# Clustered attention into a gated MLP: second projection's weights staged later, low parts on POOL, more buffers, sums on PE

## The chip, the cores and the metric

One Trainium2 chip, one core. The time is that of one execution on the device, in microseconds; lower is better. The core has five engines that run side by side and wait for each other by semaphores: PE (TensorE, matmul), DVE (VectorE), ACT (ScalarE), POOL (GpSimd) and SP (SyncE, which here only issues DMAs). PEld is PE's weight load, which overlaps its matmuls. Every engine works through its own list of instructions in the order of the list: an instruction that waits holds up all that stand behind it.

## The reference

Shapes: q, k, v are (batch 4, heads 8, sequence 768, head size 64); there are 16 centroids per head.

```python
q_assign = np.argmax(np.einsum('bhsd,hcd->bhsc', q_n, c_n), axis=-1)   # normalised q, k, centroids
k_assign = np.argmax(np.einsum('bhsd,hcd->bhsc', k_n, c_n), axis=-1)
mask = q_assign[:, :, :, None] == k_assign[:, :, None, :]
scores = np.where(mask, scale * np.matmul(q, k.transpose(0, 1, 3, 2)), -1000000000.0)
attn = np.exp(scores - np.max(scores, axis=-1, keepdims=True))
attn = attn / (np.sum(attn, axis=-1, keepdims=True) + 1e-09)
x = np.matmul(attn, v)                                   # heads side by side: (4, 768, 512)

h = np.maximum(x @ w_in, 0.0)                            # w_in (512, 1024)
u, v = (h[..., :d_ff // 2], h[..., d_ff // 2:])          # 512 columns each
v_n = (v - mu) / np.sqrt(var + 1e-06)                    # over the 512 columns
v_s = np.einsum('ts,bsd->btd', w_spatial, v_n) + b_spatial[None, :, None]
return ((u * v_s) @ w_out).astype(np.float32)            # w_out (512, 512)
```

w_in and w_out arrive as 64-bit floats, which DVE turns into 32-bit ones by three instructions on their 32-bit words.

## The kernel before, in words

**Numbers.** Nearly every matmul operand is held as two f16 parts, a high part (the value rounded to f16) and a low part (the value less the high part), and a product is three matmuls: high by high, high by low, low by high. So each tile that feeds PE costs a cast on one engine and a subtraction on another. ACT mostly makes the high parts, and POOL or DVE the low ones.

**Attention.** The 32 heads go in 16 pairs; pairs 0 to 3 are the first batch, 4 to 7 the second. For a pair, `prep` loads `raw` (k and q, transposed) and `vraw`, splits them into `hq`/`lo` (L532 on ACT, L538 on DVE) and `vhl` (L601 on ACT, L606 on DVE; for the first two pairs L604 on POOL), assigns clusters on DVE (L566 to L578), and forms the column sums of v that the rows without a key in their cluster need. These sums come in two ways. For pairs 0 to 3 PE multiplies a tile of ones with the split v (L613 and L614, 12 matmuls). For later pairs (`short`) DVE adds the six blocks of `vraw` into `vs` (L621), and PE adds over the partitions in one f32 matmul (L622). `shifts` computes scores once for their row maxima: PE L662 into a PSUM bank `acc`, DVE's maximum `nm` (L669), 18 to a head. `attend` then does for each of a head's six key tiles the scores (PE, L713 and L715, into `sc`), exp (ACT, L719, `p`), the high part (ACT, L721) and the low part (POOL, L722) of `pt`, and the values (PE, L727, 18 matmuls). A head ends with DVE's `rc` (L746), the first instruction on its finished values: there are 32, and the texts count progress by them. `xhl` is the head's result as two parts, and a DMA turns a pair's into `xT`.

**MLP.** For a batch, `mlp` makes six v tiles (12 matmuls each against the second half of `win`; ACT's relu into `v32`, DVE's mean and variance L798 to L812, `vn` in two parts, the low one by POOL, L813), six u tiles (first half of `win`), six s tiles (18 matmuls against `wsp`, then DVE's L832, L833 and POOL's L834, and a DMA that transposes `ghl` into `gT`) and six p tiles (12 matmuls against `wou`, ACT's L842 into `o32`, and an output DMA that ACT issues, L843). All big MLP matmuls have line L771 (a helper). MLP tiles of a batch are spread among the next batch's attention; the last batch's have nothing to stand among.

**Weights.** `weights` (from L450) stages a weight: load; for the 64-bit ones DVE's L477, L478, L479 (into `top`, which for `w_in` is a PSUM bank `acc`); ACT's L461 for the high part; DVE's L462 for the low part. `w_in` is loaded into the buffer that later holds `vn`, four tiles for its second half (columns of v), then four for its first (columns of u). `early_weights` gives times for its loads from `W_AT` on, `W_GAP` apart; `late_weights` stages `wsp` (12 tiles) and `wou` (8 tiles) from `WL_AT` on.

**Order.** The kernel plans its own order. `Plan.run` goes through the operations by estimated costs, and at each free engine takes, of those that are ready, the one with the lowest `due` time plus `key`. The result is one fixed list for each engine, in which the SP queue (nearly all loads, and the transposes) is one more in-order list. Whoever changes a cost, a key or a number of buffers changes the lists everywhere.

**Buffers.** `o32` has 1, `v32` 2 (`MV_BUFS`), `u32` 4; `acc` four PSUM banks and `sc` two double ones. PE, DVE's maxima, the MLP and the staging of `w_in` share the four banks.

Of the kernel before, what the change touches and what calls it, by code (L numbers as in the profile page):

```python
# [69 lines left out]
K_RC = -1.64  # L70
K_XD = 3.66
K_X = -1.98
K_VT = -3.58
K_G = -9.5
KP0 = -16.99
# [200 lines left out]
def kernel(  # L276
# [175 lines left out]
    def weights(jobs, at, gap, key, raws, tops, on, after=()):  # L452
        ends = []
        for m, (src, dst, n, lg, wide, cell) in enumerate(jobs):
# [3 lines left out]

            def lows(x, ld, n=n, dst=dst, sc=sc, raw=raw, cell=cell, use=()):

                h = op("ACT", 0.2 + 0.00085 * n, lambda: A.activation(out=dst()[:, 0, :], in_=x(), func=AF.Copy, scale=sc), after=ld, use=use, key=key)  # L461
                lo = op("DVE", (0.05 if n > 384 else 0.4) + 0.00125 * n, lambda: V.scalar_tensor_tensor(out=dst()[:, 1, :], in0=x(), scalar=sc, in1=dst()[:, 0, :], op0=ALU.mult, op1=ALU.subtract), after=[h], use=use, key=key)  # L462
                w_ops.setdefault(cell, []).extend([h, lo])
                ends.append(lo)
# [51 lines left out]
    def prep(n):  # L516
# [98 lines left out]

        short = n >= NPR
        m = D if short else D + 1
        unit = MEAN_UNIT * (V_SCALE if short else 1.0)
        if short:
            vs = r_vs.new()  # L620
            o = op("DVE", 0.9, lambda: V.tensor_reduce(out=vs.t, in_=vraw.t.rearrange("p t c -> p c t"), axis=AX.X, op=ALU.add), after=[ldv], use=[vraw], new=[vs], key=KV)  # L621
            o = op("PE", 0.4, lambda: T.matmul(out=sv.t[0:2, 0:2 * (D + 2)].rearrange("p (h d) -> p h d", h=2)[:, :, 0:D], lhsT=one32, rhs=vs.t.rearrange("p (h d) -> p h d", h=2), start=True, stop=True), after=[o, c_wh], use=[vs], new=[sv], cols=512, key=KV)  # L622
# [136 lines left out]
    vn_read = [[] for _ in range(NT)]  # L759

    def mlp(b):
        plan.due = None
# [25 lines left out]
        def v_tile(t, pos):  # L788
# [21 lines left out]
            for k, t, v in ((0, t - 1, vs[0]), (1, t, vs[1])):  # L810
                o = op("DVE", 0.62, lambda k=k, v=v: V.tensor_scalar(out=v.t, in0=v.t, scalar1=mv.t[:, k, 0:1], scalar2=y.t[:, k:k + 1], op0=ALU.subtract, op1=ALU.mult), after=[yo], use=[v, mv, y], key=1)
                h = op("DVE", 0.41, lambda t=t, v=v: V.tensor_copy(out=vn[:, 0, t, :], in_=v.t), after=[o] + vn_read[t], use=[v], key=1)  # L812
                l = op("POOL", 1.3, lambda t=t, v=v: G_.tensor_tensor(out=vn[:, 1, t, :], in0=v.t, in1=vn[:, 0, t, :], op=ALU.subtract), after=[h], use=[v], key=1)  # L813
# [23 lines left out]
        def p_tile(t, tr, pos):  # L837
# [4 lines left out]
            o = op("ACT", 0.57, lambda: A.activation(out=o32.t, in_=acc.t, func=AF.Copy, scale=2.0 ** -(G_LOG + WOUT_LOG)), after=[o], use=[acc], new=[o32], key=-0.7)  # L842
            op("ACT", 0.06, lambda: A.dma_start(out=out[b, t * P:(t + 1) * P, :], in_=o32.t), after=[o], use=[o32], dma=0.8, key=0)  # L843

# [69 lines left out]
```

## Time and profile before

| what | us |
|---|---|
| median of 3 runs (690.49 to 691.19) | 691.05 |
| the profiled execution | 694.26 |
| its span, first to last instruction | 692.5 |
| PE, DVE, ACT, POOL busy in the span | 637.5, 482.0, 437.7, 435.3 |
| mean granted PE clock | 0.985 |

The profiled execution is one of its own, 3.2 us longer than the median of the runs. The page lists a matmul's whole duration, and matmuls are pipelined: an instruction that is listed with 379 ns is followed by the next after 216 ns. So a busy PE need not be a full PE; what PE could do is better read from how fast matmuls follow each other where nothing holds them. DVE's and ACT's listed durations also overlap, by less. The granted clock counts for PE alone.

### The profile page before, as it was taken

How to read it: one execution, taken by the hardware profiler on the slowest of the kernel's cores; microseconds unless marked ns; L12 is line 12 of the kernel's file. 1: busy time of each engine (PE TensorE's matmuls, PEld its weight loads, DVE VectorE, ACT ScalarE, POOL GpSimd, SP SyncE). 2: the span in 40 equal slices, each digit the busy share in tenths (PEclk: the TensorE clock that was granted, in tenths of full speed). 3: DMA queues.
4: the chain of work that ended last, by engine and by line, in shares of the span. 5: the costliest groups of instructions: out<-in, count | busy, mean ns of one | idle time of the engine just before them, and what ended most of it. 6: DMA issues, size and time to landing. Idle time of an engine off the chain costs nothing.

```text
span 692.5 us, 16725 instructions
## 1 busy us (share of the span) xinstructions
PE 637.5 (92%) x6757; PEld 379.0 (55%) x6757; DVE 482.0 (70%) x940; ACT 437.7 (63%) x685; POOL 435.3 (63%) x305
## 2 busy tenths in 40 slices
PE   2978889999998999988799899999999999999996
PEld 1456566666555655555445556556655655544442
DVE  6999989998969889999754877558485821215210
ACT  5686889998848756678443966667673957412111
POOL 2485778998949667677363976767665966703210
PEclk9998999999999799999999999999999999999999
DMA  5567665574634467442831536262510113140223
GB/s 165 147 154 213 147 107 142 137 168 116 138 110 82 97 165 167 109 116 60 189 61 36 150 74 137 61 152 50 120 34 1 37 28 70 32 115 0 31 61 92
DMA packets 106515, 70.49 MB, mean 102 GB/s; under 512 B 90379, under 2 KB 93126, under 8 KB 106438
## 3 DMA queue, kind: packets, MB, share of 16 engines
q1 hardware_dynamic: 102694, 62.74, 40.4%
q10 hardware_dynamic: 3744, 6.69, 2.7%
q8 instruction: 53, 0.87, 0.5%
q14 instruction: 24, 0.20, 0.1%
HBM read 27.63 MB, written 6.29 MB: 49 GB/s over the span
## 4 chain that ended last, share of the span: by engine, by line
PE 60%; DVE 20%; ACT 9%; issue 5%; DMA 4%; POOL 2%; POOLq 0%; SPq 0%; ACTq 0%; DVEq 0%
PE acc L771 35%; PE acc L727 9%; DVE nm L669 8%; PE acc L662 6%; PE sc L713 5%; PE sc L715 5%; ACT p L719 4%; ACT pt L721 3%; DVE lo L538 2%; POOL pt L722 2%; DMA out_dram<-o 2%; DMA gT<-ghl 1%; ACT hq L532 1%; DVE vhl L606 1%; DVE acc L568 1%
## 5 line engine op out<-in xcount | busy, mean ns | idle before, releaser
L722 POOL TENSOR_TENSOR pt<-p,pt 128x768 f16<-128x768 f32 x192 | 329.7, 1736 | 103.1 <-ACT pt L721 50.6
L719 ACT ACTIVATE p<-sc,plog 128x768 f32<-128x768 f32 x192 | 168.9, 898 | 58.4 <-PE sc L715 53.8
L669 DVE TENSOR_REDUCE nm<-acc 128x1 f32<-128x512 f32 (+1 forms) x288 | 179.8, 683 | 12.4 <-PE acc L662 12.0
L721 ACT CAST pt<-p 128x768 f16<-128x768 f32 x192 | 155.6, 828 | 12.9 <-PE acc L727 11.1
L727 PE MATMUL acc<-vhl,pt 128*128 128x65 f16 (+1 forms) x3456 | 139.2, 196 | 7.6 <-POOL pt L722 6.9
L727 PEld LDWEIGHTS <-pt 128*128 128x128 f16 x3456 | 129.1, 99 | 30.3 <-POOL pt L722 10.1
L771 PE MATMUL acc<-win,xT 128*128 128x512 f16 x576 | 130.0, 379 | 0.0
L662 PE MATMUL acc<-hq 80*128 80x256 f16 (+1 forms) x384 | 101.1, 339 | 20.7 <-DVE nm L669 10.1
L713 PE MATMUL sc<-hq,lo 128*128 128x512 f16 (+1 forms) x384 | 95.7, 331 | 6.3 <-ACT p L719 6.1
L715 PE MATMUL sc<-hq 81*128 81x512 f16 (+1 forms) x384 | 96.0, 331 | 1.0 <-DMA hq<-sht 1.0
L771 PE MATMUL acc<-vn,wsp 128*128 128x512 f16 x432 | 96.8, 379 | 0.0
L771 PEld LDWEIGHTS <-xT 128*128 128x128 f16 x576 | 54.9, 98 | 63.2 <-issue 0.7
L771 PEld LDWEIGHTS <-wsp 128*128 128x128 f16 x432 | 41.8, 98 | 48.9 <-issue 0.2
L834 POOL TENSOR_TENSOR ghl<-u,ghl 128x512 f16<-128x512 f32 x24 | 27.7, 1156 | 64.0 <-DVE ghl L833 49.2
L832 DVE SCALAR_TENSOR_TENSOR u<-acc,bsp,u 128x512 f32<-128x512 f32 x24 | 17.9, 747 | 71.5 <-PE acc L771 71.5
L771 PE MATMUL acc<-wou,gT 128*128 128x512 f16 x288 | 65.6, 379 | 1.7 <-DMA gT<-ghl 1.7
L662 PEld LDWEIGHTS <-hq 80*128 80x128 f16 x384 | 35.3, 99 | 43.2 <-issue 25.1
L538 DVE SCALAR_TENSOR_TENSOR lo<-raw,hq 128x768 f16<-128x768 f32 x30 | 44.9, 1505 | 12.4 <-ACT hq L532 12.0
L713 PEld LDWEIGHTS <-lo 128*128 128x128 f16 x384 | 34.1, 98 | 34.9 <-issue 20.8
L715 PEld LDWEIGHTS <-hq 81*128 81x128 f16 x384 | 37.9, 99 | 27.7 <-issue 2.7
L842 ACT ACTIVATE o<-acc 128x512 f32<-128x512 f32 x24 | 14.3, 597 | 57.0 <-PE acc L771 41.2
L771 PEld LDWEIGHTS <-gT 128*128 128x128 f16 x288 | 27.7, 98 | 33.8 <-DMA gT<-ghl 2.2
(111 smaller groups left out, 628.5 us busy)
## 6 DMA issues: line engine op xcount, KB each, us to landing
raw<-in_kqT_dram SPq DMA_DIRECT2D x15, 768.0 KB
vraw<-in_vp_dram SPq DMA_DIRECT2D x16, 384.0 KB
out_dram<-o ACTq DMA_DIRECT2D x24, 256.0 KB
hq<-hq SPq DMA_DIRECT2D x15, 384.0 KB
vn<-in_w_in_dram SPq DMA_DIRECT2D x8, 512.0 KB
hq<-lo SPq DMA_DIRECT2D x16, 192.0 KB
lo<-hq SPq DMA_DIRECT2D x16, 192.0 KB
wraw<-in_wsT_dram SPq DMA_DIRECT2D x12, 192.0 KB
```

The lines of the kernel that those rows point to most:

```text
L538: los.append(op("DVE", 1.4 if n else 0.96, lambda h=h: V.scalar_tensor_tensor(out=lo.t[:, h, :], in0=raw.t[:, h, :], scalar=QK_SCALE, in1= ...
L662: T.matmul(out=acc.t[:, c:c + cs.stop - cs.start], lhsT=hq.t[0:R_SH, 1, h, t * P:(t + 1) * P], rhs=hq.t[0:R_SH, 0, h, cs], start=c == 0, s ...
L669: V.tensor_reduce(out=nm.t[:, t, k:k + 1] if n == 1 else nm.t[:, t:t + n, k], in_=src, axis=AX.X, op=ALU.max, negate=True)
L713: T.matmul(out=sc.t[:, cs], lhsT=lo.t[:, h, ks], rhs=hq.t[:, 2, h, cs], start=True, stop=False)
L715: T.matmul(out=sc.t[:, cs], lhsT=hq.t[0:R_E, 0, h, ks], rhs=hq.t[0:R_E, 1, h, cs], start=False, stop=True)
L719: o = op("ACT", 0.9, lambda sc=sc, p32=p32: A.activation(out=p32.t, in_=sc.t[:, 0:S], func=AF.Exp, bias=plog, scale=SC_UNIT), after=[o, m_ ...
L721: o = op("ACT", 0.83, lambda pt=pt, p32=p32: A.copy(out=pt.t[:, 0, :], in_=p32.t), after=[o], use=[p32], new=[pt], key=K_HI)
L722: o = op("POOL", 1.72, lambda pt=pt, p32=p32: G_.tensor_tensor(out=pt.t[:, 1, :], in0=p32.t, in1=pt.t[:, 0, :], op=ALU.subtract), after=[o ...
L727: T.matmul(out=av.t[:, t * (D + 1):t * (D + 1) + w], lhsT=lhsT, rhs=rhs, skip_group_check=True, **f)
L771: T.matmul(out=acc.t, lhsT=lr[m][0], rhs=lr[m][1], start=(m == 0), stop=(m == n - 1))
L832: o = op("DVE", 0.72, lambda: V.scalar_tensor_tensor(out=u32.t, in0=acc.t, scalar=bsp[:, t:t + 1], in1=u32.t, op0=ALU.add, op1=ALU.mult), ...
L834: l = op("POOL", 1.2, lambda: G_.tensor_tensor(out=ghl.t[:, 1, :], in0=u32.t, in1=ghl.t[:, 0, :], op=ALU.subtract), after=[h], use=[u32, g ...
```

## The change

- `early_weights` gets a second time: the tiles of the second half of `w_in` (v) load from `W_AT` on, those of the first half (u) from `W2_AT` on. Since the loads use `vn`'s buffer, the first batch's `vn` now waits for the end of both (`staged`).
- The low parts of `wsp` go from one DVE instruction (L462) to two: ACT scales the loaded tile in place, and POOL subtracts the high part.
- `o32` has 2 buffers, `v32` 3.
- `short` begins at pair 8: pairs 4 to 7 take their sums of v on PE, and DVE's `vs` and the f32 matmul fall away for them.
- Four estimates of cost are changed, and most of the keys and due times. The instructions of the attention and of the MLP stay what they were, in another order.

```diff
-MV_BUFS = 2
+MV_BUFS = 3
-W_KEY = 7.7
-WL_KEY = 0.91
-W_AT = 28.34
-W_GAP = 5.52
+W_KEY = 5.13
+WL_KEY = 1.28
+W_AT = 26.85
+W2_AT = 112.97
+W_GAP = 5.89
...
-K_LO = 2.77
+K_LO = 6.27
...
-    r_o32 = R(moe, "o32", [P, DM], F32, 1)
+    r_o32 = R(moe, "o32", [P, DM], F32, 2)
...
                 h = op("ACT", 0.2 + 0.00085 * n, lambda: A.activation(out=dst()[:, 0, :], in_=x(), func=AF.Copy, scale=sc), after=ld, use=use, key=key)
-                lo = op("DVE", (0.05 if n > 384 else 0.4) + 0.00125 * n, lambda: V.scalar_tensor_tensor(out=dst()[:, 1, :], in0=x(), scalar=sc, in1=dst()[:, 0, :], op0=ALU.mult, op1=ALU.subtract), after=[h], use=use, key=key)
+                if not wide:
+                    o = op("ACT", 0.2 + 0.00085 * n, lambda: A.activation(out=x(), in_=x(), func=AF.Copy, scale=sc), after=[h], use=use, key=key)
+                    lo = op("POOL", 0.1 + 0.0021 * n, lambda: G_.tensor_tensor(out=dst()[:, 1, :], in0=x(), in1=dst()[:, 0, :], op=ALU.subtract), after=[o], use=use, key=key)
+                else:
+                    lo = op("DVE", (0.05 if n > 384 else 0.4) + 0.00125 * n, lambda: V.scalar_tensor_tensor(out=dst()[:, 1, :], in0=x(), scalar=sc, in1=dst()[:, 0, :], op0=ALU.mult, op1=ALU.subtract), after=[h], use=use, key=key)
...
     def early_weights():
-        jobs = []
-        for hf in (1, 0):
+        ends = []
+        for hf, at in ((1, W_AT), (0, W2_AT)):
+            jobs = []
...
-        return weights(jobs, W_AT, W_GAP, W_KEY, r_wraw0, r_acc, "SP")
+            ends += weights(jobs, at, W_GAP, W_KEY, r_wraw0, r_acc, "SP")
+        return ends
...
-        short = n >= NPR
+        short = n >= 2 * NPR
...
+    def staged():
+        return w_ops[("win", 0)] + w_ops[("win", 1)]
...
-                h = op("DVE", 0.41, lambda t=t, v=v: V.tensor_copy(out=vn[:, 0, t, :], in_=v.t), after=[o] + vn_read[t], use=[v], key=1)
+                h = op("DVE", 0.41, lambda t=t, v=v: V.tensor_copy(out=vn[:, 0, t, :], in_=v.t), after=[o] + vn_read[t] + (staged() if b == 0 else []), use=[v], key=1)
```

What the lists show of it, at three places. First DVE, at the end of the fourth head. Before, the last two tiles of the u half stand there (`acc<-vn` are the three word instructions, `win` the low part), in front of the head's `rc`:

```order
L477 TENSOR_SCALAR acc_114<-vn 128x512
L477 TENSOR_SCALAR acc_113<-vn 128x512
L478 SCALAR_TENSOR_TENSOR acc_114<-vn,acc_114 128x512
L478 SCALAR_TENSOR_TENSOR acc_113<-vn,acc_113 128x512
L479 SCALAR_TENSOR_TENSOR acc_114<-vn,acc_114 128x512
L479 SCALAR_TENSOR_TENSOR acc_113<-vn,acc_113 128x512
L462 SCALAR_TENSOR_TENSOR win<-acc_114,win 128x512
L462 SCALAR_TENSOR_TENSOR win<-acc_113,win 128x512
L746 TENSOR_SCALAR rc<-acc_115 128x6
```

In the change the same instructions (with new line numbers: L482 to L484 and L467) stand around the `rc` of the eighth head, among a later pair's maxima `nm`:

```order
L676 TENSOR_REDUCE nm_91<-acc_112 128x1
L482 TENSOR_SCALAR acc_115<-vn 128x512
L676 TENSOR_REDUCE nm_91<-acc_113 128x2
L483 SCALAR_TENSOR_TENSOR acc_115<-vn,acc_115 128x512
L482 TENSOR_SCALAR acc_113<-vn 128x512
L484 SCALAR_TENSOR_TENSOR acc_115<-vn,acc_115 128x512
L483 SCALAR_TENSOR_TENSOR acc_113<-vn,acc_113 128x512
L545 SCALAR_TENSOR_TENSOR lo<-raw,hq 128x768
L484 SCALAR_TENSOR_TENSOR acc_113<-vn,acc_113 128x512
L753 TENSOR_SCALAR rc<-acc_114 128x6
L467 SCALAR_TENSOR_TENSOR win<-acc_115,win 128x512
```

The u half has moved from the third and fourth heads to the seventh to ninth. Second, POOL at the twelfth head, where the first batch's v tiles are normalised (`vn`). Before:

```order
L813 TENSOR_TENSOR vn<-v_3351,vn 128x512
L813 TENSOR_TENSOR vn<-v_3387,vn 128x512
L722 TENSOR_TENSOR pt<-p_3506,pt 128x768
L805 TENSOR_TENSOR y<-a,mhalf 128x2
L722 TENSOR_TENSOR pt<-p_3559,pt 128x768
L722 TENSOR_TENSOR pt<-p_3581,pt 128x768
L813 TENSOR_TENSOR vn<-v_3489,vn 128x512
```

In the change (L729 is `pt`, L816 `y`, L824 `vn`, L465 the moved low part):

```order
L824 TENSOR_TENSOR vn<-v_3361,vn 128x512
L824 TENSOR_TENSOR vn<-v_3386,vn 128x512
L465 TENSOR_TENSOR wsp<-wraw,wsp 128x384 x2
L816 TENSOR_TENSOR y<-a,mhalf 128x2
L465 TENSOR_TENSOR wsp<-wraw,wsp 128x384
L824 TENSOR_TENSOR vn<-v_3486,vn 128x512
L824 TENSOR_TENSOR vn<-v_3520,vn 128x512
L465 TENSOR_TENSOR wsp<-wraw,wsp 128x384
L729 TENSOR_TENSOR pt<-p_3601,pt 128x768
L729 TENSOR_TENSOR pt<-p_3626,pt 128x768
L465 TENSOR_TENSOR wsp<-wraw,wsp 128x384
```

Five of the twelve stand before the twelfth head's last `pt`, all twelve before the fourteenth's. Third, ACT at the first batch's p tiles. Before, three results stand with one exp among them:

```order
L842 ACTIVATE o_5517<-acc_114 128x512
L843 DMA out_dram<-o_5517 128x512
L842 ACTIVATE o_5577<-acc_113 128x512
L843 DMA out_dram<-o_5577 128x512
L719 ACTIVATE p_5584<-sc_111,plog 128x768
L721 CAST pt<-p_5584 128x768
L842 ACTIVATE o_5636<-acc_112 128x512
L843 DMA out_dram<-o_5636 128x512
```

In the change (L853 and L854 are the result and its DMA, L726 exp, L728 the high part, L688 and L691 small rows of the shift):

```order
L853 ACTIVATE o_5091<-acc_112 128x512
L854 DMA out_dram<-o_5091 128x512
L853 ACTIVATE o_5108<-acc_113 128x512
L854 DMA out_dram<-o_5108 128x512
L726 ACTIVATE p_5164<-sc_110,plog 128x768
L728 CAST pt<-p_5164 128x768
L688 ACTIVATE shx_86<-nl 128x6
L691 ACTIVATE shx_86<-nl,flag 128x6 x2
L726 ACTIVATE p_5211<-sc_111,plog 128x768
L728 CAST pt<-p_5211 128x768
L757 CAST xhl<-xn 128x6x64
L853 ACTIVATE o_5233<-acc_113 128x512
```

Two results still stand in a row, but with two buffers the second needs no landing of the first, and the third stands two exps further on. The first p tiles also come earlier: ACT's first result stands in the eighteenth head instead of the nineteenth.

More of the change, by code (lines that the diff above doesn't have):

```diff
@@ L42 @@
 DUE = 25.06
-DUE_PREP = -1.8
+DUE_PREP = -1.88
 DUE_MAX = -0.66
-DUE_M = 31.24
+DUE_M = 31.37
 DUE_W = 1.2
@@ L49 @@
 V_BUFS = 2
-MV_BUFS = 2
+MV_BUFS = 3
 U_BUFS = 4
 MM = 6
-W_KEY = 7.7
-WL_KEY = 0.91
-WL_AT = 183.98
-WL_GAP = 3.25
-W_AT = 28.34
-W_GAP = 5.52
-PREP_KEY = 2.81
-AV_KEY = 1.09
-K_SC = -2.4
+W_KEY = 5.13
+WL_KEY = 1.28
+WL_AT = 183.63
+WL_GAP = 3.35
+W_AT = 26.85
+W2_AT = 112.97
+W_GAP = 5.89
+PREP_KEY = 2.55
+AV_KEY = 1.25
+K_SC = -2.21
 K_MX = -2.81
-K_MAX = -0.27
+K_MAX = -2.18
 TBL = 0.14
-K_SH = -3.11
-K_EXP = 0.71
-K_HI = -1.78
-K_LO = 2.77
[L70 to L74, printed above, removed]
+K_SH = -3.05
+K_EXP = -0.75
+K_HI = -1.44
+K_LO = 6.27
+K_RC = -2.97
+K_XD = 3.02
+K_X = -3.85
+K_VT = -2.01
+K_G = -9.74
 KP0 = -16.99
@@ L457, in weights, with lows @@
             t0 = at + gap * m
-            def lows(x, ld, n=n, dst=dst, sc=sc, raw=raw, cell=cell, use=()):
+            def lows(x, ld, n=n, wide=wide, dst=dst, sc=sc, raw=raw, cell=cell, use=()):
                 h = op("ACT", 0.2 + 0.00085 * n, lambda: A.activation(out=dst()[:, 0, :], in_=x(), func=AF.Copy, scale=sc), after=ld, use=use, key=key)
-                lo = op("DVE", (0.05 if n > 384 else 0.4) + 0.00125 * n, lambda: V.scalar_tensor_tensor(out=dst()[:, 1, :], in0=x(), scalar=sc, in1=dst()[:, 0, :], op0=ALU.mult, op1=ALU.subtract), after=[h], use=use, key=key)
+                if not wide:
[3 more added lines that the diff above has]
+                    lo = op("DVE", (0.05 if n > 384 else 0.4) + 0.00125 * n, lambda: V.scalar_tensor_tensor(out=dst()[:, 1, :], in0=x(), scalar=sc, in1=dst()[:, 0, :], op0=ALU.mult, op1=ALU.subtract), after=[h], use=use, key=key)
                 w_ops.setdefault(cell, []).extend([h, lo])
@@ L537, in prep @@
                 continue
-            los.append(op("DVE", 1.4 if n else 0.96, lambda h=h: V.scalar_tensor_tensor(out=lo.t[:, h, :], in0=raw.t[:, h, :], scalar=QK_SCALE, in1=hq.t[:, 0, h, :], op0=ALU.mult, op1=ALU.subtract), after=[his[h]], use=[raw, hq] + ([lo] if h else []), new=[] if h else [lo], key=KP))
+            los.append(op("DVE", 1.45 if n else 0.96, lambda h=h: V.scalar_tensor_tensor(out=lo.t[:, h, :], in0=raw.t[:, h, :], scalar=QK_SCALE, in1=hq.t[:, 0, h, :], op0=ALU.mult, op1=ALU.subtract), after=[his[h]], use=[raw, hq] + ([lo] if h else []), new=[] if h else [lo], key=KP))
         if n == 0:
-            qa0 = [op("ACT", 0.75, lambda x=x: A.copy(out=hq.t[0:D, x], in_=hq.t[D:P, 0]), after=his, use=[hq], key=KP) for x in (1, 2)]
+            qa0 = [op("ACT", 1.47, lambda x=x: A.copy(out=hq.t[0:D, x], in_=hq.t[D:P, 0]), after=his, use=[hq], key=KP) for x in (1, 2)]
         else:
@@ L620, in prep @@
             vs = r_vs.new()
-            o = op("DVE", 0.9, lambda: V.tensor_reduce(out=vs.t, in_=vraw.t.rearrange("p t c -> p c t"), axis=AX.X, op=ALU.add), after=[ldv], use=[vraw], new=[vs], key=KV)
+            o = op("DVE", 1.45, lambda: V.tensor_reduce(out=vs.t, in_=vraw.t.rearrange("p t c -> p c t"), axis=AX.X, op=ALU.add), after=[ldv], use=[vraw], new=[vs], key=KV)
             o = op("PE", 0.4, lambda: T.matmul(out=sv.t[0:2, 0:2 * (D + 2)].rearrange("p (h d) -> p h d", h=2)[:, :, 0:D], lhsT=one32, rhs=vs.t.rearrange("p (h d) -> p h d", h=2), start=True, stop=True), after=[o, c_wh], use=[vs], new=[sv], cols=512, key=KV)
@@ L842, in p_tile @@
             o = op("ACT", 0.57, lambda: A.activation(out=o32.t, in_=acc.t, func=AF.Copy, scale=2.0 ** -(G_LOG + WOUT_LOG)), after=[o], use=[acc], new=[o32], key=-0.7)
-            op("ACT", 0.06, lambda: A.dma_start(out=out[b, t * P:(t + 1) * P, :], in_=o32.t), after=[o], use=[o32], dma=0.8, key=0)
+            op("ACT", 0.06, lambda: A.dma_start(out=out[b, t * P:(t + 1) * P, :], in_=o32.t), after=[o], use=[o32], dma=3.0, key=0)
         u_ops = {}
```

## The prediction

> **What bounds the kernel now.** I read first the page, then busy time by stretch, cut where heads end (at DVE's `rc`, once per head, so the cuts are the ends of heads 1, 8, 11, 12, 13, 17, 19, 20, 21 and 32), and then the chain of waits inside the stretches that have a hole.
>
> ```profile
> span 692.5 us, 16725 instructions
> PE 637.5 (92%) x6757; PEld 379.0 (55%) x6757; DVE 482.0 (70%) x940; ACT 437.7 (63%) x685; POOL 435.3 (63%) x305
> PE 60%; DVE 20%; ACT 9%; issue 5%; DMA 4%; POOL 2%; POOLq 0%; SPq 0%; ACTq 0%; DVEq 0%
> ```
>
> PE looks like the bound of everything. The stretches tell it differently (busy us and instructions of each engine, then granted PE clock, DMA share, GB/s):
>
> ```profile
> core 0: us, PE busy (x) PEld busy (x) DVE busy (x) ACT busy (x) POOL busy (x), PEclk, DMA share, GB/s
> 49.00:145.50 96.50, 83.05 (x1223) 58.80 (x1222) 92.72 (x173) 83.59 (x136) 76.12 (x48) 0.95 0.65 157
> 145.50:183.50 38.00, 35.39 (x507) 23.86 (x506) 35.00 (x63) 36.12 (x58) 34.84 (x23) 1.00 0.61 124
> 183.50:216.00 32.50, 32.30 (x306) 17.70 (x305) 25.39 (x54) 19.94 (x35) 20.69 (x15) 1.00 0.36 103
> 216.00:238.60 22.60, 18.84 (x172) 11.42 (x170) 20.76 (x34) 16.85 (x26) 18.16 (x12) 0.77 0.56 101
> 238.60:311.30 72.70, 69.19 (x822) 42.70 (x819) 68.94 (x118) 49.79 (x79) 48.08 (x31) 1.00 0.55 138
> 311.30:341.20 29.90, 25.66 (x331) 15.88 (x328) 24.90 (x41) 18.72 (x30) 19.56 (x13) 1.00 0.52 119
> 341.20:387.90 46.70, 44.05 (x349) 23.18 (x348) 25.25 (x59) 24.65 (x41) 24.12 (x19) 1.00 0.27 61
> 387.90:403.90 16.00, 14.52 (x177) 9.56 (x174) 15.91 (x31) 14.59 (x22) 15.82 (x11) 1.00 0.58 151
> 403.90:603.10 199.20, 197.94 (x2165) 118.33 (x2164) 110.11 (x216) 126.98 (x195) 135.52 (x94) 1.00 0.33 68
> 603.10:692.50 89.40, 84.17 (x390) 37.80 (x387) 21.77 (x56) 13.65 (x23) 18.64 (x18) 1.00 0.25 58
> ```
>
> Up to 183.5 us (the first batch's attention, with the second's beginning) DVE is busy 127.7 of 134.5 us, and in the second row ACT (36.12 of 38) and POOL (34.84) stand beside it. From 183.5 to 216 (the first batch's v and u tiles) PE is full, DVE has 7 us free. From 216 to 311 DVE is full again (89.7 of 95.3). From 403.9 on it is PE: 197.94 of 199.2, then the last batch's MLP. So time can be won before 404 us, where PE waits for others; what follows moves up as a block.
>
> ```profile
> 59.81 1.20 DVE acc L479 x2
> ...
> 113.99 1.52 DVE vs L621
> ...
> 219.84 1.80 DVE wsp L462
> 222.11 1.44 DVE wsp L462
> ...
> 330.34 4.57 DMA out_dram<-o
> 335.63 6.43 DMA out_dram<-o
> ...
> 602.92 72.53 PE acc L771 x336
> 675.52 4.68 DMA gT<-ghl
> ...
> 686.19 2.78 PE acc L771 x12
> ```
>
> These rows of the chain name what stands in the holes: word instructions of the weights, `vs`, the spatial low parts, the one result buffer. The end is 72.53 us of matmuls at 0.216 us, and a wait for the last transposes that no edit touches.
>
> **The change part by part.** *The u half.* A tile of it costs DVE four instructions at 0.60 us (1.20 for two, above), 2.4 us, so 9.6 us for four, and ACT four casts. They leave the third and fourth head for the seventh to ninth. Both places lie ahead of the eleventh `rc`, in the stretch in which DVE is 95% busy: counted in DVE's list up to there, no u instruction is missing or added. So the end of that stretch wins nothing by the move as such; the early heads become shorter, the eighth and ninth longer. I take 0; it is between −3 (half of the 6.8 us of idle DVE in the first two rows, if the load is spread better) and +3 (ACT and POOL, both over 90% in the second row, start later there). The first batch's `vn` now waits for these tiles, but stands in the twelfth head, behind a full PE stretch: 0, and if the tiles ran that late, one tile's 2.4 us.
>
> *The second batch's sums.*
>
> ```profile
> L621 DVE TENSOR_REDUCE vs<-vraw 128x128 f32<-128x768 f32 x12 | 18.0, 1498 | 0.8 <-DMA vraw<-in_vp_dram 0.8
> 115.56 0.38 PE L622 MATMUL acc<-vs,one 128*2 128x128 f32 x2 [0.34 <-DVE vs L621]
> 65.75 0.32 PE L613 MATMUL acc<-vhl,ones 128*128 128x130 f16 x1
> ...
> 66.95 0.31 PE L614 MATMUL acc<-vhl,ones 128*128 128x128 f16 x1
> 95.78 0.22 PE L613 MATMUL acc<-vhl,ones 128*128 128x130 f16 x1
> ...
> 96.42 0.22 PE L614 MATMUL acc<-vhl,ones 128*128 128x128 f16 x1
> ```
>
> Four `vs` leave DVE, 6.0 us: three ahead of the eleventh `rc` (4.5 us), one in the stretch where PE is full (nothing). PE gets 12 matmuls a pair, from the first row to the last one's start 0.64 us at full pace and 1.20 at half, for two that take 0.38: some +0.3 to +0.9 a pair, 1 to 4 us in all. Most of it falls where PE idles (13.45 us in the first row). I take −4 and +1; ends −5 and 0 for the one, 0 and +4 for the other.
>
> *The spatial low parts.*
>
> ```profile
> L462 DVE SCALAR_TENSOR_TENSOR wsp<-wraw,wsp 128x384 f16<-128x384 f32 x12 | 11.3, 938 | 2.0 <-ACT wsp L461 2.0
> L462 DVE SCALAR_TENSOR_TENSOR wsp<-wraw,wsp x12: 535/556/1953, 195.0 to 244.5; 128x384 f16<-128x384 f32 x12
> L461 ACT ACTIVATE wsp<-wraw 128x384 f16<-128x384 f32 x12 | 6.2, 518 | 0.8 <-DMA wraw<-in_wsT_dram 0.7
> L751 POOL TENSOR_TENSOR xhl<-xn,xhl 128x384 f16<-128x384 f32 x32 | 32.7, 1023 | 5.2 <-ACT xhl L750 5.1
> 216.00:224.00 8.00, 5.29 (x49) 3.12 (x46) 7.95 (x11) 6.34 (x10) 8.00 (x6) 0.86 0.73 96
> 224.00:232.00 8.00, 7.48 (x63) 4.58 (x61) 6.61 (x12) 4.50 (x7) 5.86 (x4) 0.50 0.65 152
> ```
>
> DVE loses 11.3 us. Seven of the twelve stood ahead of the twelfth `rc`, under the full PE: nothing won. Five (4.7 us) stood behind it, two of them in the chain with 1.80 and 1.44. ACT gets 12 copies like L461 (6.2 us), POOL 12 subtractions of `xhl`'s size (12.3 us). Five of POOL's lie in the PE-full stretch, which has 11.8 us of POOL and 12.6 of ACT free; the other seven come among `pt` (the low part of the exps) in heads 13 and 14, where POOL at 216 to 224 has nothing free. There PE falls to a clock of 0.50 for 8 us once it has starved, so a microsecond of delay there costs up to two. I take −3; −7 if all 4.7 go through and the clock recovers some, +3 if POOL's `pt` come late by three subtractions.
>
> A rule of the Trainium skill bears on this (SBUF — State Buffer, section Who interferes with whom): a DVE instruction with two SBUF inputs and a GpSimd one that reads SBUF exclude each other for a whole instruction, while one with at most one SBUF input does not contend. The trace agrees: the same instruction takes 0.535 to 1.953 us.
>
> *More buffers.* ACT's two waits for the single `o32`:
>
> ```profile
> 335.00 0.60 ACT L842 ACTIVATE o<-acc 128x512 f32<-128x512 f32 x1 [4.69 <-DMA out_dram<-o]
> 342.16 0.60 ACT L842 ACTIVATE o<-acc 128x512 f32<-128x512 f32 x1 [4.32 <-DMA out_dram<-o]
> ACT v L792 <- POOL vn L813: 22.8, 8, 4.2
> ```
>
> Behind each wait stand exps, so the attention stops: ACT loses 9.0 us. PE has matmuls meanwhile; it idles 4.2 us of 311.3 to 341.2 and 2.7 of the next stretch. With two buffers, and the results further apart, the waits go; next in line is DVE, 24.90 of 29.9. I take −4, between 0 and −6.9. The third `v32` ends part of ACT's 22.8 us of waits, but those lie where PE is full: 0.
>
> *Order.* Elsewhere the lists differ in detail. After the 21st `rc` (403.9) PE's rows come in nearly the same order, and the 390 matmuls of the last batch are the same: 0.
>
> Sum: 0 − 4 + 1 − 3 − 4 = −10, from 694.3 for the profiled execution to 684.3; the median of the runs lies 3.2 lower, so **681 us**.
>
> **The rivals.** *(a) Everything counts.* DVE's list shrinks by 17.3 us (6.0 + 11.3); if every stretch before 404 follows DVE and the stop at the results goes too (6.9), it is 24, with PE's extra work 22: 669. For it: DVE's 95%. Against: half of the spatial parts lay under PE. *(b) Hidden anyway.* ACT and POOL hold the second row as it is, PE has other work in the stops: −1, 690. For it: 36.12 and 34.84 of 38. Against: the first row, where they have 13 and 20 us free. *(c) The exclusion changes sides.* Twelve POOL instructions more that read SBUF meet DVE's other two-input ones (`lo`, the words of the third weight), and what DVE won is blocked again: the twelve were blocked for 11.3 − 12 × 0.535 = 4.9 us, now on others. The −3 becomes +2, 686. This is what the skill's rule above would make of it. *(d) Slower: POOL becomes the bound in heads 13 and 14.* Its seven new subtractions, 7.2 us, stand in front of `pt`; in 216 to 238.6 POOL has 4.4 us free, so 2.8 are late, doubled by the fallen clock to 5.6; and the key that puts `pt` behind other POOL work delays values in the first batch too, where POOL has 3.2 us free of 38 and each late `pt` (1.7 us) repeats, say in six heads: 10 us. With the −4 of the results and the −4 of the sums +8: 699. It decides once POOL in 145.5 to 183.5 has no idle left. Against it: in the first two rows POOL does the same number of instructions as before.
>
> **How the numbers follow.** The forecast has a chance of 0.50 (its own range 676 to 687), (a) 0.12, (b) 0.13, (c) 0.10, (d) 0.15. From 670 to 693 nearly all of the forecast, (b) and (c) lie inside, half of (a) and a third of (d): about 0.8 with some error of my own. A measurement tells 0.2% (1.4 us) from no change. Faster: the forecast, (a), (c) and a part of (b), 0.76; the same: the rest of (b), 0.09; slower 0.15.
>
> **What would show it.** The eighth and eleventh `rc` 3 to 5 us earlier than 145.5 and 183.5; DVE still over 90% busy up to there; the twelfth 4 us earlier, no more; no wait of ACT for `out_dram` near 330; the twentieth some 10 us earlier than 387.9; the rest from there as long as before. Wrong would be: an eleventh `rc` no earlier (b), POOL full in heads 9 to 14 with PE's clock below 0.8 (d), DVE's `lo` longer than now (c), or a stretch after 404 us of another length.

## The result, and the profile after

The change takes 683.83 us (median of 4 runs, 682.75 to 684.47), the kernel before 691.12 beside it (690.49 to 693.33): the ratio is 0.9882, with a 95% interval of 0.9856 to 0.9908. It is 1.2% faster, 2.8 us above the 681 that was forecast and inside the range.

The profiled executions differ by more than the medians, 694.26 against 682.75 us: the one of before is slower than any of the four runs timed beside the change, the one of the change the fastest of its four. So the traces are read place by place. The page of the change:

```profile
span 680.9 us, 16824 instructions
PE 631.2 (93%) x6797; PEld 377.7 (55%) x6797; DVE 467.5 (69%) x924; ACT 441.9 (65%) x697; POOL 442.4 (65%) x317
```

DVE lost 14.5 us of work, ACT got 4.2 and POOL 7.1. Busy time by stretch, cut at the same heads as in the prediction (ends of heads 1, 8, 11, 12, 13, 17, 19, 20, 21 and 32; the columns are those named there):

```profile
core 0: us, PE busy (x) PEld busy (x) DVE busy (x) ACT busy (x) POOL busy (x), PEclk, DMA share, GB/s
54.30:138.60 84.30, 73.83 (x1151) 53.34 (x1148) 81.66 (x149) 78.83 (x125) 74.06 (x46) 0.96 0.65 152
138.60:178.50 39.90, 37.30 (x570) 26.64 (x569) 37.27 (x72) 38.32 (x62) 35.59 (x23) 1.00 0.65 139
178.50:210.30 31.80, 30.92 (x278) 16.70 (x276) 22.89 (x49) 20.35 (x37) 25.01 (x21) 1.00 0.43 108
210.30:226.70 16.40, 14.54 (x205) 10.20 (x203) 15.71 (x31) 15.57 (x28) 16.40 (x13) 1.00 0.49 117
226.70:307.40 80.70, 72.96 (x789) 43.41 (x789) 72.72 (x114) 51.26 (x86) 49.00 (x34) 0.98 0.58 136
307.40:343.50 36.10, 34.89 (x410) 21.64 (x408) 29.47 (x53) 29.11 (x45) 29.03 (x20) 1.00 0.59 136
343.50:376.60 33.10, 33.10 (x292) 17.85 (x291) 14.79 (x46) 16.51 (x27) 17.11 (x15) 1.00 0.10 28
376.60:393.60 17.00, 15.82 (x183) 10.12 (x181) 16.79 (x32) 16.18 (x24) 17.00 (x11) 1.00 0.47 104
393.60:591.20 197.60, 196.50 (x2160) 117.66 (x2158) 108.10 (x217) 126.48 (x194) 134.40 (x94) 1.00 0.39 73
591.20:680.90 89.70, 84.35 (x390) 37.89 (x388) 21.89 (x56) 13.64 (x23) 18.84 (x18) 1.00 0.26 58
```

Against before, the eighth `rc` comes 6.7 us earlier, the eleventh 4.9, the twelfth 5.5, the thirteenth 11.7, the seventeenth only 3.7, the twentieth 11.2; from there to the end it is 304.3 us after 304.7. The first head ends 5.5 us later (54.3 after 48.8).

A cut at an `rc` does not always enclose the same work, since MLP tiles are moved between heads. So I also reckoned PE's **lost time**: of each stretch its length less the work of the matmuls that start in it, each taken at a round 2,400 columns a microsecond (512 in 0.213 us; in the traces 512 columns follow each other every 0.215 us at the fastest, 0.216 in the last tiles, so about 1% of all work counts as lost without a wait), very short ones at 0.030 us. A lower clock counts as lost. The span is the work and the lost time. One profiled execution each, in us; e1 to e12 are the experiments below:

```
              work   head 1   2-11   12-13   14-17   18-20   21-end   lost in all
before       597.2     26.4   31.0    10.3     5.3     8.4     13.8      95.3
the change   598.1     29.1   22.4     4.3    11.3     2.4     13.5      82.9
e1           598.1     30.4   22.9     4.3    11.3     3.1     11.1      83.1
e2           598.1     29.1   22.1     5.5     8.5     7.2     13.6      86.0
e3           598.1     29.6   27.0     5.1     5.4     6.5     14.5      88.2
e4           597.2     29.8   28.8     5.6    15.0     1.4     12.2      92.8
e5           597.2     29.6   28.2     6.4    13.3     3.7     12.3      93.3
e6           598.1     25.9   39.3     4.7     6.7     4.6     14.2      95.4
e7           597.2     27.9   31.0     8.5     5.3     6.2     14.0      92.8
e8           598.1     29.6   22.1     4.2     4.0     1.7     13.0      74.6
e9           597.2     26.4   31.6     8.5     3.3     2.8     13.4      86.0
e10          597.2     30.5   27.9     5.3     6.8     2.5     11.6      84.6
e11          598.9     30.0   22.1     4.1    10.1     1.9     12.2      80.5
e12          598.1     29.4   22.1     4.5    14.1     1.4     12.8      84.4
```

The gain stands in heads 2 to 11 (8.6 us) and 12 to 13 (6.0, of which 1.8 belong to that execution of before: e7 and e9, with the same order up to there, lose 8.5). The first head loses 2.7 us more than before. One list, executed twice, differs by up to 1.8 us at a place (before and e7 in heads 1 to 13), so less than that says nothing. In heads 14 to 20 change and before lose the same, 13.7 us, only at other places.

Where heads 14 to 17 lose it stands in ACT's and DVE's waits (whole execution: us in total, times, longest), of the kernel before and of the change:

```profile
ACT o L842 <- DMA out_dram<-o: 15.9, 4, 4.7
...
ACT wou L461 <- DVE top L479: 10.3, 5, 4.0
```

```profile
ACT o L853 <- PE acc L782: 42.9, 17, 5.9
...
ACT wou L462 <- DVE top L484: 16.4, 6, 4.0
...
DVE wou L467 <- ACT wou L462: 4.1, 3, 3.1
```

The waits for `out_dram` at the results are gone. ACT's waits for the third weight's words (`top`) grew from 10.3 to 16.4. One of them in the change's timeline (start, duration):

```profile
273.63 6.68 POOL L729 TENSOR_TENSOR pt<-p,pt 128x768 f16<-128x768 f32 x4
...
277.20 1.62 DVE L482 TENSOR_SCALAR top<-wraw 128x256 uint32<-128x256 uint32 x1
278.86 1.74 DVE L483 SCALAR_TENSOR_TENSOR top<-wraw,top 128x256 uint32<-128x256 uint32 x1
280.52 0.74 DVE L843 SCALAR_TENSOR_TENSOR u<-acc,bsp,u 128x512 f32<-128x512 f32 x1
281.19 0.41 DVE L484 SCALAR_TENSOR_TENSOR top<-wraw,top 128x256 uint32<-128x256 uint32 x1
...
281.63 0.42 ACT L462 ACTIVATE wou<-top 128x256 f16<-128x256 f32 x1 [3.99 <-DVE top L484]
...
282.54 0.29 DVE L482 TENSOR_SCALAR top<-wraw 128x256 uint32<-128x256 uint32 x1
282.86 0.42 DVE L483 SCALAR_TENSOR_TENSOR top<-wraw,top 128x256 uint32<-128x256 uint32 x1
...
282.89 0.48 PE L720 MATMUL sc<-hq,lo 128*128 128x512 f16 x2 [3.40 <-ACT p L726]
```

POOL runs four `pt` without a gap; DVE's word instructions last 1.62 and 1.74 us beside them, and 0.29 and 0.42 once they are through; ACT stands 3.99 us behind them, and PE 3.40 us behind the exp that waits in ACT's list.

### The profile page after: what moved, and what is told of

Read it like the earlier page. It is cut to its first block, busy times and chain, and to the rows that moved or that the text cites. A ratio compares the mean times of both kernels' runs of the same rounds, so it can differ in the third digit from the quotient of the medians.

```text
span 680.9 us, 16824 instructions
## 1 busy us (share of the span) xinstructions
PE 631.2 (93%) x6797; PEld 377.7 (55%) x6797; DVE 467.5 (69%) x924; ACT 441.9 (65%) x697; POOL 442.4 (65%) x317
## 5 line engine op out<-in xcount | busy, mean ns | idle before, releaser
L729 POOL TENSOR_TENSOR pt<-p,pt 128x768 f16<-128x768 f32 x192 | 326.7, 1720 | 71.0 <-ACT pt L728 48.0
L726 ACT ACTIVATE p<-sc,plog 128x768 f32<-128x768 f32 x192 | 168.4, 896 | 47.2 <-PE sc L722 44.8
L728 ACT CAST pt<-p 128x768 f16<-128x768 f32 x192 | 155.6, 827 | 8.7 <-PE acc L734 6.9
L734 PE MATMUL acc<-vhl,pt 128*128 128x65 f16 (+1 forms) x3456 | 135.1, 193 | 9.9 <-POOL pt L729 9.7
L734 PEld LDWEIGHTS <-pt 128*128 128x128 f16 x3456 | 125.4, 98 | 32.2 <-POOL pt L729 12.2
L669 PE MATMUL acc<-hq 80*128 80x256 f16 (+1 forms) x384 | 97.4, 337 | 10.4 <-DVE nm L676 5.5
L845 POOL TENSOR_TENSOR ghl<-u,ghl 128x512 f16<-128x512 f32 x24 | 29.1, 1211 | 72.6 <-DVE ghl L844 64.5
L545 DVE SCALAR_TENSOR_TENSOR lo<-raw,hq 128x768 f16<-128x768 f32 x30 | 46.6, 1559 | 8.1 <-ACT hq L539 8.0
L824 POOL TENSOR_TENSOR vn<-v,vn 128x512 f16<-128x512 f32 x24 | 28.9, 1219 | 21.1 <-DVE vn L823 21.1
```

The source lines that it names most:

```text
L545: los.append(op("DVE", 1.45 if n else 0.96, lambda h=h: V.scalar_tensor_tensor(out=lo.t[:, h, :], in0=raw.t[:, h, :], scalar=QK_SCALE, in1 ...
L669: T.matmul(out=acc.t[:, c:c + cs.stop - cs.start], lhsT=hq.t[0:R_SH, 1, h, t * P:(t + 1) * P], rhs=hq.t[0:R_SH, 0, h, cs], start=c == 0, s ...
L726: o = op("ACT", 0.9, lambda sc=sc, p32=p32: A.activation(out=p32.t, in_=sc.t[:, 0:S], func=AF.Exp, bias=plog, scale=SC_UNIT), after=[o, m_ ...
L728: o = op("ACT", 0.83, lambda pt=pt, p32=p32: A.copy(out=pt.t[:, 0, :], in_=p32.t), after=[o], use=[p32], new=[pt], key=K_HI)
L729: o = op("POOL", 1.72, lambda pt=pt, p32=p32: G_.tensor_tensor(out=pt.t[:, 1, :], in0=p32.t, in1=pt.t[:, 0, :], op=ALU.subtract), after=[o ...
L734: T.matmul(out=av.t[:, t * (D + 1):t * (D + 1) + w], lhsT=lhsT, rhs=rhs, skip_group_check=True, **f)
```

## The experiments

Each with the median of its runs, their range and number, the ratio to the kernel before on the same chip, and its interval. All compute everything. The change stands at 0.9882.

**e1: one result buffer.**

```diff
-    r_o32 = R(moe, "o32", [P, DM], F32, 2)
+    r_o32 = R(moe, "o32", [P, DM], F32, 1)
```

> The changed kernel with one result buffer again (all else, the numbers too, as in the change; the lists are planned anew). Theory S (the gain is a sum of the parts, each in its stretch): the two waits for the output DMA come back, 4 us slower than the change, 687 to 689; in the trace a wait of 4 us or more of ACT for the output DMA. Theory O (the new keys and times make the gain, the parts themselves little): within 1.5 us of the change, 683 to 685.

683.06 us (681.17 to 683.77, 4), 0.9867 [0.9837, 0.9898]: as fast as the change, as theory O had it. With the change's order two results wait, 5.1 us in all:

```profile
ACT o L853 <- DMA out_dram<-o: 5.1, 2, 3.6
```

**e7: two result buffers in the kernel before.** The same line, from 1 to 2.

> The kernel before with two result buffers and nothing else. Theory S: the two waits of ACT near 330 us (9.0 us) go, 3 to 6 us faster than before, 685 to 688. Theory O: within 1.5 us of before, 690 to 693.

691.38 us (689.80 to 692.66, 10), 1.0006 [0.9989, 1.0022]. That is theory O's range. ACT's waits for `out_dram` at the results are gone from the trace: 9.0 us in heads 18 to 20, which are the two waits of the prediction, and 6.9 in the last batch's MLP. But ACT's waits for PE at the same results grew; before, then e7:

```profile
ACT o L842 <- PE acc L771: 41.2, 14, 5.9
...
ACT o L842 <- PE acc L771: 51.3, 18, 5.9
```

In heads 18 to 20 they went from 4.4 to 9.0 us, so half of the 9.0 only changed its name. These heads lose 2.2 us less in that one execution, hardly more than one list differs by itself, and the median does not move. The second buffer is worth nothing that the medians show, in either kernel.

**e2: the spatial low parts back on DVE.**

```diff
-                if not wide:
+                if False:
```

> The changed kernel with the spatial low parts on DVE again (one instruction there, none on POOL, no second ACT copy). Theory S: 3 to 6 us slower than the change, 687 to 690, with the loss behind the twelfth head. Theory O: 683 to 685. The exclusion changing sides (rival c): no slower, 682 to 685, and DVE's lo and the third weight's words get shorter by as much as the twelve cost.

686.93 us (685.85 to 687.41, 5), 0.9931 [0.9905, 0.9957]: 3.1 us above the change, just below theory S's range. Its heads 12 and 13:

```profile
178.20:211.00 32.80, 32.12 (x284) 17.30 (x283) 28.81 (x55) 19.96 (x35) 22.18 (x16) 1.00 0.47 117
211.00:229.60 18.60, 16.26 (x250) 12.23 (x250) 18.23 (x35) 16.36 (x26) 15.94 (x10) 0.91 0.56 144
```

DVE is full again in head 13 (18.23 of 18.6), the clock falls to 0.91, and the thirteenth `rc` comes 2.9 us later. Part of that is MLP work that lies earlier (45.8 us in the two heads instead of 43.9); lost are 1.2. DVE's other instructions of the kind that rival (c) names (`lo`, `vhl`, the words and the low part of `wou`) take 86.5 us here after 91.5 in the change, but in e3 and e4, with the twelve still on POOL, they take 85.9 and 85.1: a new plan moves this sum by as much, so it does not decide on (c).

**e3: the u half early again.**

```diff
-W2_AT = 112.97
+W2_AT = 50.41
```

> The changed kernel with the u half loaded right after the v half (from 50.4 us instead of 113.0). Theory S: the place doesn't matter within the stretch in which DVE is full: 682 to 686, eleventh rc within 2 us of the change's 178.5. Against it, if the later staging is what gains: 688 to 691, eleventh rc at 182 to 184.

688.12 us (685.62 to 692.35, 6), 0.9954 [0.9921, 0.9987]: 4.3 us above the change: the later staging does gain, and the eleventh `rc` is later than either theory had it. Heads 2 to 5 and 6 to 11 of e3, then of the change:

```profile
54.40:111.60 57.20, 48.96 (x714) 34.48 (x712) 55.78 (x106) 50.99 (x81) 44.98 (x28) 0.92 0.70 163
111.60:184.80 73.20, 66.09 (x1029) 47.58 (x1026) 64.56 (x119) 68.38 (x109) 67.60 (x41) 1.00 0.65 134
```

```profile
54.30:103.00 48.70, 42.33 (x656) 30.66 (x653) 47.11 (x89) 44.43 (x71) 39.61 (x25) 0.93 0.62 144
103.00:178.50 75.50, 68.79 (x1065) 49.33 (x1064) 71.82 (x132) 72.72 (x116) 70.03 (x44) 1.00 0.67 150
```

With u early, DVE is full in heads 2 to 5 (55.78 of 57.2) and has 8.6 us free in 6 to 11, where ACT and POOL are fuller. With u late, DVE is nearly full in both parts (47.11 of 48.7, 71.82 of 75.5). The eleventh `rc` is 6.3 us later in e3, 4.6 of it lost time.

**e4: the second batch's sums on DVE again.**

```diff
-        short = n >= 2 * NPR
+        short = n >= NPR
```

> The changed kernel with the second batch's sums on DVE again. Theory S: 4 us slower than the change, 686 to 689, eleventh rc 3 to 5 us later than 178.5. Theory O: 683 to 685.

692.02 us (688.88 to 694.49, 10), 1.0002 [0.9980, 1.0023]: all of the change's gain is gone, more than either theory had. 6.4 us of lost time come back in heads 2 to 11 (the eleventh `rc` at 185.8), 3.7 more in 14 to 17, a place to which the prediction gave nothing of the sums. With the u half late and the sums on DVE, it is DVE that is fullest in heads 6 to 11:

```profile
104.40:185.80 81.40, 70.77 (x1039) 48.82 (x1038) 76.66 (x137) 74.80 (x118) 71.61 (x45) 0.98 0.68 148
```

**e10: both undone**, e3's line and e4's.

> The changed kernel with both undone: u half early and the second batch's sums on DVE. Theory S (each part gains by itself, here 4.3 and 8.2 us): 694 to 698, eleventh rc at 190 or later. Theory J (the two gain only together: the late u half fills the DVE time that the sums leave free in heads 6 to 9): 687 to 692, like either alone, eleventh rc at 183 to 187.

684.69 us (681.45 to 686.34, 4), 0.9887 [0.9849, 0.9924]. The eleventh `rc` comes at 186.3: undoing both costs there what undoing either does (5.5 us lost, after 4.6 and 6.4). So the two parts earn that gain together, as theory J had it. Its heads 6 to 11:

```profile
113.20:186.30 73.10, 66.63 (x1026) 46.88 (x1024) 64.88 (x121) 69.01 (x108) 66.52 (x41) 0.98 0.61 134
```

With the u half early DVE has 8.2 us free there though the sums are on it, as it has 8.6 in e3 without them. But the end is as early as the change's, which neither theory had: heads 14 to 17 lose 4.5 us less than in the change.

**e5: the numbers alone** (keys, due times, load times and the four estimates of cost of the change in the kernel before; no part moved).

```diff
-DUE_PREP = -1.8
+DUE_PREP = -1.88
...
-W_GAP = 5.52
-PREP_KEY = 2.81
-AV_KEY = 1.09
+W_GAP = 5.89
+PREP_KEY = 2.55
+AV_KEY = 1.25
...
-K_LO = 2.77
+K_LO = 6.27
```

> The kernel before with the change's numbers alone (keys, due times, load times and the four cost estimates; one result and two v buffers, both halves of the first weight from one time on, spatial low parts on DVE, sums on DVE from the second batch on). Theory S (the parts make the gain): 689 to 693. Theory O (the numbers make it): 683 to 686.

693.12 us (692.11 to 696.14, 5), 1.0039 [1.0016, 1.0061]: slightly slower, a little above theory S's range. The late end of the first head (54.7) comes with the numbers.

**e6: the parts alone** (the u half late, sums on PE, low parts on POOL, buffers; every other number as before).

```diff
+W2_AT = 112.97
...
-    r_o32 = R(moe, "o32", [P, DM], F32, 1)
+    r_o32 = R(moe, "o32", [P, DM], F32, 2)
...
-        short = n >= NPR
+        short = n >= 2 * NPR
```

> The change's parts alone (buffers, second staging time, spatial low parts on POOL, second batch's sums on PE) with the numbers of before. Theory S: 681 to 686. Theory O: 689 to 693.

696.59 us (695.24 to 696.96, 4), 1.0074 [1.0058, 1.0089]: slower too, which neither theory had. The eighth `rc` is 4.7 us earlier than before (140.6), the eleventh 14.6 later (198.0). 7.5 us of that are MLP work that now lies ahead of it, and heads 9 to 11 lose some 10 us more than before, at a low clock:

```profile
140.60:198.00 57.40, 49.93 (x594) 33.15 (x595) 48.48 (x94) 38.59 (x64) 37.74 (x24) 0.85 0.56 132
```

**e8: the words of the third weight in PSUM**, in the change. They go into a bank `acc`, as those of `w_in` do, instead of `top`, and their estimated costs fall to those of `w_in`'s.

```diff
-    r_top = R(wk, "top", [P, 256], F32, 1)
...
-... out=top.t.bitcast(U32) ...
+... out=top.t[:, :n].bitcast(U32) ...
...
-        weights(jobs, WL_AT, WL_GAP, WL_KEY, r_wraw, r_top, "SP", after)
+        weights(jobs, WL_AT, WL_GAP, WL_KEY, r_wraw, r_acc, "SP", after)
```

> The changed kernel with the third weight's words put together in a PSUM bank (as the first weight's are) instead of in SBUF, and DVE's cost estimates for them set to those of the first weight's. In the change's trace these 32 DVE instructions take 28.4 us (743, 1318, 720 and 770 ns each kind) and heads 14 to 17 give back 8 us. If that is DVE instructions and POOL shutting each other out, each of the 32 falls to 0.3 to 0.45 us, DVE gains some 16 us in the stretch from the 13th to the 17th rc, and the kernel gets 3 to 8 us faster than the change, 676 to 681. If DVE is not what holds heads 14 to 17, or the bank is missed more, 683 to 687.

674.53 us (674.49 to 674.64, 4), 0.9758 [0.9744, 0.9773]: the fastest kernel here, 9.3 us below the change and faster than expected. Groups of instructions (busy, mean ns, idle before), of the change and of e8:

```profile
L483 DVE SCALAR_TENSOR_TENSOR top<-wraw,top 128x256 uint32<-128x256 uint32 x8 | 10.5, 1318 | 0.1
...
L467 DVE SCALAR_TENSOR_TENSOR wou<-top,wou 128x256 f16<-128x256 f32 x8 | 6.2, 770 | 4.1 <-ACT wou L462 4.1
L482 DVE TENSOR_SCALAR top<-wraw 128x256 uint32<-128x256 uint32 x8 | 5.9, 743 | 0.1
L484 DVE SCALAR_TENSOR_TENSOR top<-wraw,top 128x256 uint32<-128x256 uint32 x8 | 5.8, 720 | 0.1
```

```profile
L482 DVE SCALAR_TENSOR_TENSOR acc<-wraw,acc 128x256 uint32<-128x256 uint32 x8 | 3.4, 421 | 0.1
...
L481 DVE TENSOR_SCALAR acc<-wraw 128x256 uint32<-128x256 uint32 x8 | 3.4, 421 | 0.0
L466 DVE SCALAR_TENSOR_TENSOR wou<-acc,wou 128x256 f16<-128x256 f32 x8 | 3.4, 419 | 3.7 <-ACT wou L461 3.7
```

The 32 instructions take 13.5 us instead of 28.4. That POOL is what held them shows in the two traces. In the change the two-input ones take 0.40 to 0.42 us in the eleven cases without a POOL instruction beside them and 0.66 to 1.88 in the thirteen with one; in e8 they take 0.41 to 0.43 in both cases, here beside three `pt`:

```profile
237.62 5.56 POOL L728 TENSOR_TENSOR pt<-p,pt 128x768 f16<-128x768 f32 x3
...
238.40 0.41 DVE L482 SCALAR_TENSOR_TENSOR acc<-wraw,acc 128x256 uint32<-128x256 uint32 x1
```

ACT's wait in e8, which was 16.4 us, and then its heads 14 to 17:

```profile
ACT wou L461 <- DVE acc L483: 6.0, 3, 3.2
```

```profile
226.90:306.80 79.90, 77.66 (x844) 46.25 (x844) 63.71 (x124) 56.11 (x92) 51.85 (x36) 1.00 0.64 150
```

In these heads DVE is busy 63.71 us instead of 72.72, PE fits 844 matmuls in instead of 789, and the lost time falls from 11.3 us to 4.0. The e8 edit also replans the lists, so not all of the 9.3 us need be the words'.

**e9: the same in the kernel before.**

> The kernel before with the third weight's words in a PSUM bank (and its DVE cost estimates to match), nothing else. If DVE and POOL shut each other out there in the kernel before as well (26.2 us of DVE for these 32 instructions), 4 to 9 us faster than before, 682 to 687. If the change brought the exclusion on by putting more on POOL, less than 3 us: 688 to 692.

685.42 us (683.97 to 686.31, 4), 0.9901 [0.9878, 0.9924]. Heads 14 to 20 lose 6.1 us instead of 13.7. So the words were blocked before as well (the 32 instructions take 26.2 us there, 13.3 in e9), and the change did not bring that on.

**e11: e8 with the third batch's sums on PE as well.**

```diff
-        short = n >= 2 * NPR
+        short = n >= 3 * NPR
```

> The changed kernel with the third weight's words in PSUM and the third batch's sums on PE too. Four vs (6.0 us) leave DVE in heads 13 to 20, where DVE is full (with the words in SBUF); PE gets some 2 us. If DVE still sets the pace there: 2 to 4 us faster than with the words alone, 670 to 673; if PE or ACT do by now: 674 to 677.

681.26 us (677.89 to 684.15, 4), 0.9841 [0.9790, 0.9892]: slower than e8 by 6.7, which neither range had, though DVE has a little less to do (452.4 us after 453.3). PE gets 0.8 us of work more; heads 14 to 17 lose 10.1 us instead of 4.0. What paid in heads 2 to 11 does not pay here; whether the sums or the new plan lose the 6 us is not shown, since e12 moves by nearly as much.

**e12: one key alone** in the change, to see what a mere replanning does.

```diff
-AV_KEY = 1.25
+AV_KEY = 1.09
```

> The changed kernel with one key of the values matmuls (AV_KEY) back at its number from before, 1.25 to 1.09; every part stays. What planning anew does by itself: within 2 us of the change, 682 to 686. If it moves more than that, single parts worth 3 to 4 us can't be read from kernels that were planned anew.

688.85 us (683.86 to 696.25, 10; without the longest 687.96, up to 693.73), 0.9947 [0.9914, 0.9980]: 4 to 5 us above the change, where at most 2 were expected. Up to the eleventh `rc` the trace is the change's, and the thirteenth comes at 226.1 after 226.7; heads 14 to 17 lose 14.1 us after 11.3, 18 to 20 lose 1.4 after 2.4. Its profiled execution is as long as the change's (a span of 682.4), while its runs spread over 10 us even without the longest; I have no cause for that. So a difference of 3 to 5 us at the end between two plans is not the price of the part in which they differ. e2 and e3 have such differences, and for them only the places count.

## Why the prediction was right, and where it was not

**The sum** was −10; the medians gave −7.3, the profiled pair −11.5. The stretches that were named as the bound were the right ones: from the 20th `rc` on only 0.4 us was won, and PE's work rose by 0.9 us in the reckoning above, where +1 was taken for the sums. That the sum lies so near is in part luck. By the thirteenth `rc` the profiled pair had won 11.7 us, where the terms gave 6; in heads 14 to 20, where they gave 4 more, it won nothing (149.9 us after 149.3). What came too much in the one place made up for what did not come in the other.

**The signs it named.** The eleventh `rc` (4.9 us earlier) and the twentieth (11.2) came as stated, the rest is as long as before within 0.4 us, DVE is busy 118.9 of 124.2 us up to the eleventh, no result waits for `out_dram`. The eighth came earlier than stated (6.7), the twelfth a little (5.5 where "4 us earlier, no more" stood).

**The u half, "0", and the second batch's sums, "−4".** Together right in size at the eleventh `rc`, wrongly divided. Heads 2 to 11, all with the change's numbers, take:

```
                 sums on DVE     sums on PE
u half early     130.6 (e10)     130.4 (e3)
u half late      131.1 (e4)      124.2 (the change)
```

Each part alone wins nothing, both win 6 to 7 us. The step that failed is "in the stretch in which DVE is 95% busy: … the end of that stretch wins nothing by the move as such". In the kernel before, DVE is as busy in heads 2 to 5 as in 6 to 11, but in the second ACT and POOL stand beside it:

```profile
49.00:113.90 64.90, 53.50 (x748) 37.89 (x747) 61.33 (x116) 54.00 (x88) 46.26 (x30) 0.92 0.66 159
113.90:183.50 69.60, 64.94 (x987) 44.77 (x984) 66.40 (x121) 65.71 (x105) 64.69 (x40) 1.00 0.63 136
```

With the u half early ACT and POOL are busier there than DVE (e3, e10), and taking the sums off DVE shortens nothing. The late u half shortens heads 2 to 5 by some 8 us in either case (57.2 to 48.7, and 57.5 to 49.7). It lengthens heads 6 to 11 by 2.3 us where the sums have left DVE (73.2 to 75.5) and by 8.3 where they have not (73.1 to 81.4). So the sums make the room that the u half needs. The term of 0 was mis-sized beyond its bound of −3, and the −4 is not the sums' by themselves. It takes the numbers too: with those of before, the same two parts come to 149.7 us (e6).

**The spatial low parts, "−3".** e2 gives +3.1 when they go back, with 1.2 us of lost time at heads 12 and 13. The sign and the size agree; that the 3.1 is theirs is not shown, for the reason in e12 and because 1.2 us at a place is less than one list differs by itself. Nor are most of the 6.0 us that heads 12 to 13 won theirs: e2 loses 5.5 there, and e5, with none of the parts, 6.4, after 10.3 before (8.5 in e7 and e9).

**The results' buffer, "−4".** This term failed: the medians show nothing, twice (e1, e7). The step was to take ACT's waits as time of the attention, with DVE next in line. In e7 it is PE that is next: ACT's waits for PE at the results grow by 10.1 us where 15.9 of waits for the DMA go, and at the place itself at most 2.2 us are won. The 6 us less that heads 18 to 20 lose in the change do not need the second buffer (e1 loses 3.1 there, the change 2.4, before 8.4), and 14 to 17 lose 6 us more.

**What was left out** are those 6 us in heads 14 to 17, and what the replanned lists do at large. The 0 for "Order" was stated for what follows the 21st `rc` and holds there within 1.3 us; before it the order decides. Neither the numbers (e5, +1.7 us) nor the parts (e6, +5.1) gain anything alone.

**The rivals.** (a) fell: heads 14 to 20 lose what they lost. (b) fell at the eleventh `rc`, though ACT and POOL are the busiest in heads 6 to 11 wherever the u half is early (e3, e10). (c) did not come as described: of the instructions that could be blocked, `lo` and the words got longer (by 1.7 and 3.1 us), the low part of `wou` and `vhl` shorter (by 0.9 and 4.2), and together they kept their length (91.8 us before, 91.5 after). But the same exclusion, on the words, is the largest cost that these experiments found still to be had (e8, e9), though with another plan less of it comes through (e11). The Trainium skill (SBUF — State Buffer, section Who interferes with whom) says that a DVE instruction with at most one SBUF input does not contend with GpSimd outside certain fast modes. The trace agrees: with one of two operands in PSUM the words take 0.42 us beside POOL too, where two inputs in SBUF took 0.72 to 1.32 in the mean. The prediction left the exception for those modes out. The one-input word instruction from SBUF to SBUF (L482) is held beside POOL all the same; in which mode it ran no run shows. (d) did not come: POOL is full in head 13 (16.40 of 16.40) and the clock is 1.00 there, and the head is 6.2 us shorter. DVE had been busy 20.76 of its 22.6 us before and is so for 15.71 of 16.4 now; that it had held the head, and POOL not, fits this and e2, where DVE is full again in that head (18.23 of 18.6) and the head takes 18.6 us, but e2's plan is a new one too.

**Open:** what makes the whole kernel 7 us faster. The gain up to the eleventh `rc` is that of the u half and the sums, but e10 has neither and ends as early as the change, since its heads 14 to 17 lose less. Open too: why heads 14 to 17 lose between 3.3 and 15.0 us according to the plan (the words are one cause: e8 and e9 lose least, but e11, with the words in PSUM, loses 10.1 and e3, without, 5.4); the low clock in e6's heads 9 to 11; the spread of e12's runs.

## What to carry to other kernels

Parts that work on one engine in one stretch need not add: here one makes room at a place and the other moves work into it, and neither is worth anything alone. Cut the stretch where the work goes before deciding what the move is worth, look at which engine stands beside the full one there, and try the parts singly and together. Where an in-order plan is rebuilt by every edit, judge a part by lost time at its place and first learn what a change of one number does to the end. A wait on a buffer can hide another wait that stands just behind it, and is then worth little, while a slow helper that an in-order list waits for can be worth much: here it paid to put the intermediate operand of a two-input DVE instruction into a PSUM bank while GpSimd was busy.

## What was not expected of the hardware

The same two-input 128x256 word instruction takes 0.42 us with its second operand in PSUM, beside POOL too; with it in SBUF it takes 0.72 and 1.32 us in the mean, up to 1.86 beside POOL, but 0.42 where nothing of POOL's runs beside it. The one-input instruction of the words (L482), which writes to SBUF, takes 0.27 to 0.29 us in the five cases of the change that POOL overlaps by 0.12 us or not at all, and 1.26 to 1.64 in the three beside POOL, 0.743 in the mean. When it writes to PSUM it takes 0.421: slower than the undisturbed one, but the same beside POOL. And 15.9 us of ACT's waits for a DMA, 9.0 of them in the midst of the attention, could be removed without a measurable gain (1.0006 [0.9989, 1.0022]); 10.1 us of waits for PE at the same instructions came in their place.
